# An SSM convolution in front of a gated MLP: joined products, reordered rows, a rounding moved into PSUM, and another order of the units

## The chip, the cores and the metric

The kernel runs on one core of a Trainium2 chip. TensorE (PE) multiplies matrices out of SBUF into PSUM; its weight loads are shown as an engine of their own (PEld). VectorE (DVE) and ScalarE (ACT) read and write PSUM and SBUF, GpSimd (POOL) and SyncE (SP) here mostly issue DMAs. The metric is the device time of one execution in microseconds. An execution is also profiled, and all rows below come from that one.

## The reference, cut to what matters

The input has 2048 positions and 576 channels. A first block (A) normalises each row, runs a state-space convolution along the positions and adds the result; a second block (B) is a gated MLP with a 2048x2048 mixing of the positions. Only block A is touched here.

```python
dt = exp(log_dt)[:, None];  logdA = dt * (A_re + 1j * A_im);  dB = dt * (B_re + 1j * B_im)
P  = exp(logdA[:, :, None] * arange(L))            # (576 channels, 128 states, 2048 positions)
K  = einsum("dn,dnl,dn->dl", C_re + 1j * C_im, P, dB).real
y  = irfft(rfft(pad(u)) * rfft(pad(K)))[:L] + u * Dskip     # a causal convolution per channel
...
h = layernorm(x) * (1 + ca) + sa;  x = x + ga * A(h)
h = layernorm(x) * (1 + cb) + sb;  x = x + gb * MLP(h)
```

K is a sum over 128 states of w * exp(a*l) * cos(phase*l + phi). The position l is split into a coarse and a fine part, so that K comes from products of tables. The convolution is done with a Fourier transform in stages, as matrix products.

## The kernel before, in words

The work on block A is in `ssm`, as a loop over rounds (`tick`, 0 to 39). There are 36 groups of 16 channels. In each round one group enters, and the earlier ones are each one stage further on. The units of a group g:

- `e_unit` (three groups at once, every third round): TensorE expands the logarithms of the magnitudes, a pair of products with 48 rows and 512 columns and one with 112 rows, and ScalarE takes Exp of both (lines 443 to 447) into `et`.
- `t_unit`, round g: TensorE expands the phases, counted in turns, four products of 48 rows and 256 columns into two banks of PSUM (L455). ScalarE adds a large constant, MAGIC, which rounds to whole turns (Identity, L456, into `ft`). VectorE subtracts MAGIC and the phase (L457), which leaves minus the fraction of a turn, and clears the sign into a second tile (L459).
- `s_unit`, round g+1: two Sin activations, cosine (L464) and sine (L465).
- `p_unit`, round g+2: VectorE multiplies magnitudes and phases, five instructions (L475 to L479), into `pg` and back into `et`.
- `kg_unit`, round g+3: 32 small products of 128x32 tiles into one bank (L489), copied by ScalarE with reordered columns into `kab` (L492); `d_unit` adds the skip term (L496).
- `k1_unit`, round g+4: eight products with 128x64 tiles (L506), copied by ScalarE or VectorE into `k1` (L511, L513). This is the first stage of the transform of K.

Every eight groups complete 128 channels. The input's transform runs beside it, in chunks of 512 columns. `u_unit` is one product (L548), copied by ScalarE into `ue` (L549); two DMAs of POOL's queue write `us`, the same with both halves of the partitions swapped (L551, L552). Two rounds later `z_unit` makes K's second stage (L561) and VectorE multiplies it with `ue` and with `us` (L562, L563). A round later `v_unit` transforms back with two products (L570, L571), and ScalarE's copy (L572) is stored. `y_unit` does the last stage (L615), adds x and stores.

In the first eight rounds the layer norm of block A and its first stage (`ln_pair`, L426 and L428) run in the same loop, as do the preparation of the poles and the modulation (`mod_unit`). The channel groups' pole tables (`lb`, `lc`, `la`) come by DMA from a scratch in HBM.

All these products pass through PSUM: the tiles `ps` (two, of two banks) and `pk` (four, of one bank) are handed round among the units.

What sets the order: the loop's text gives each instruction its priority, and inside the loop a scheduler puts each engine's instructions in order at build time, so they may stand otherwise than in the text. Instructions that are issued through a helper (line 145) keep the text's order; these are the parts ahead of the loop and all of the MLP behind it. Each engine then runs its list in order.

The text of a round before:

```python
go(z_unit); lag(p_unit, 2); lag(t_unit, 0); lag(s_unit, 1); go(v_unit)
lag(kg_unit, 3); go(u_unit); lag(k1_unit, 4); go(y_unit); lag(d_unit, 3)
# every third round: e_unit for three groups
```

Of the kernel before, what the change touches and what calls it, by code (L numbers as in the profile page):

```python
# [31 lines left out]
def consts():  # L32
# [64 lines left out]
    sel = np.zeros((112, 1536))  # L97
    sel[:48, :1024] = sel[64:, :1024] = half
    sel[:48, 1024:1280] = sel[64:, 1280:] = rge.reshape(48, 256)
    ones = np.zeros((128, 128))  # L100
    ones[::32] = 1.0
    f = np.float32
# [55 lines left out]
def ssm(tc, I, x1_d, consts_s, dram, mod_d, mlp):  # L158
# [5 lines left out]
    with ExitStack() as ctx:  # L164
# [22 lines left out]
        sel = tb.tile([112, 1536], BF, name="sel", bufs=1)  # L187
# [194 lines left out]
        def ln_stats(i):  # L382
            x = x4s[i]
            nm = ep.tile([128, 4], F32, name="nm")
            r = ep.tile([128, 4], F32, name="r")
            if i < 2:
                junk = ep.tile([128, 4, HC], F32, name="st1o").rearrange("p (a b) d -> p a (b d)", a=2)
                ss = ep.tile([128, 4], F32, name="ss")
# [48 lines left out]
        def e_unit(g):  # L437
            c, gi = divmod(g, 9)
            lb = lt["lb", c]
            e = et[g] = tb.tile([128, 1536], F32, name="et", bufs=5)  # L440
            pa = ps2()
            for h, (l, r) in enumerate(zip(halves(lb, gi), rows(256, 512))):
                T.matmul(pa[:, h], l, r, start=True, stop=True)
            A.activation(e[:, :1024].rearrange("p (h n) -> p h n", h=2), pa, AF.Exp)
            pb = ps1()
            T.matmul(pb, lb[:, gi], sel[:, 1024:], start=True, stop=True)
            A.activation(e[:, 1024:], pb, AF.Exp)

        def t_unit(g):
# [3 lines left out]
            for k, (n, c0) in enumerate((("lc", 768), ("la", 0))):  # L453
                for h, (l, r) in enumerate(zip(halves(lt[n, c], gi), rows(c0, 256))):
                    T.matmul(pa[:, h].rearrange("p (c k j) -> p k c j", c=8, k=2)[:, k], l, r, start=True, stop=True)  # L455
            A.activation(f, pa, AF.Identity, bias=magic)  # L456
            V.scalar_tensor_tensor(f, f, MAGIC, pa, op0=ALU.subtract, op1=ALU.subtract)  # L457
            ct = tb.tile([128, 2, 512], F32, name="ft", bufs=5)
            V.tensor_single_scalar(ct.bitcast(I32), f.bitcast(I32), 0x7FFFFFFF, op=ALU.bitwise_and)  # L459
            tt[g] = (f, ct)  # L460

        def s_unit(g):
            f, ct = tt[g]
            A.activation(ct, ct, AF.Sin, bias=halfpi, scale=-TWO_PI)  # L464
            A.activation(f, f, AF.Sin, scale=-TWO_PI)  # L465

        def p_unit(g):

            f, ct = tt[g]
            e = et.pop(g)  # L470
            p = tb.tile([128, 1536], F32, name="pg")
            pr, pi = [t[:, :1024].rearrange("p (c s j) -> p c s j", c=16, s=2) for t in (p, e)]
            gr, gi = [t[:, 1024:].rearrange("p (c a) -> p c a", c=16) for t in (p, e)]
            c3, s3 = [x.rearrange("p h (c k j) -> p k (h c) j", c=8, k=2) for x in (ct, f)]
            V.tensor_tensor(gr, gi, c3[:, 1], op=ALU.mult)  # L475
            V.tensor_tensor(pr, pi, c3[:, 0, :, None, :].to_broadcast([128, 16, 2, 32]), op=ALU.mult)
            V.tensor_tensor(gi, gi, s3[:, 1], op=ALU.mult)
            V.scalar_tensor_tensor(pi[:, :, 0], s3[:, 0], -1.0, pi[:, :, 0], op0=ALU.mult, op1=ALU.mult)
            V.tensor_tensor(pi[:, :, 1], s3[:, 0], pi[:, :, 1], op=ALU.mult)  # L479
            tt[g] = (pr, pi, gr, gi)  # L480

        def kg_unit(g):
            pr, pi, gr, gi = tt.pop(g)
            pm = ps1()
            for i in range(4):
                for x_, y_, st in ((gr, pr, True), (gi, pi, False)):
                    for j in range(4):
                        c = 4 * i + j
                        T.matmul(pm[32 * j:32 * j + 32, 64 * i:64 * i + 64], x_[:, c], y_[:, c].rearrange("p s j -> p (s j)"),  # L489
                                 start=st, stop=not st, skip_group_check=True)  # L490
            kk = kab[g] = tb.tile([128, 4, 64], F32, name="kab")
            A.activation(kk.rearrange("p i (b w) -> p i w b", w=4), pm[:, :256].rearrange("p (i w b) -> p i w b", i=4, w=4), AF.Copy)  # L492

        def d_unit(g):
            kk = kab[g]
# [34 lines left out]
        def part(n, bufs=2):  # L530
            return sb.tile([128, 512], F32, name=n, bufs=bufs)

        def by(t, c):
            return t.rearrange("p (k d) -> p k d", d=CHW[c])

# [7 lines left out]

        def u_unit(c, i):
            u1 = st.pop((c, i))
            ue = part("ue", 4)
            pm = ps1()
            T.matmul(pm, fwd, u1, start=True, stop=True)  # L548
            A.activation(ue, pm, AF.Copy)  # L549
            us = part("us", 4)  # L550
            G.dma_start(us[:64], ue[64:])  # L551
            G.dma_start(us[64:], ue[:64])  # L552
            st[c, i] = (ue, us)

        def z_unit(c, i):
            ue, us = st.pop((c, i))
            w = CHW[c]
            za, zb = part("za"), part("zb")
            pm = ps1()
            for j, k in enumerate(range(32)[kr(c, i)]):  # L560
                T.matmul(pm[:, w * j:w * j + w], cst[k // 8][:, k % 8], k1t[c][:, k, :w], start=True, stop=True)  # L561
            V.tensor_tensor(za, pm, ue, op=ALU.mult)  # L562
            V.tensor_tensor(zb, pm, us, op=ALU.mult)  # L563
            st[c, i] = (za, zb)

        def v_unit(c, i):
            za, zb = st.pop((c, i))
            v = part("ue", 4) if c == NC - 1 and i > 1 else part("v")
            pm = ps1()
            T.matmul(pm, inva, za, start=True, stop=False)  # L570
            T.matmul(pm, invb, zb, start=False, stop=True)  # L571
            A.activation(v, pm, AF.Copy)  # L572
            G.dma_start(v_d[c][:, kr(c, i)], by(v, c))

        def y_vload(c, q):
# [1 line left out]
            w = CHW[c]  # L577
            rows = v_d[c].rearrange("(b h g) k d -> b h (g k) d", b=16, h=2)[bs].rearrange("b h p d -> p h b d")
            if c == NC - 1:
                t = part("ue", 4)  # L580
                st["yv", c, q] = t[:, :4 * w], t[:, 4 * w:]
                for hh in range(2):
                    S.dma_start(by(t[:, 4 * w * hh:4 * w * hh + 4 * w], c), rows[:, hh])
                return
            if c == NC - 2 and q < 2:
                vt = [part("za"), part("zb")]
            else:
                vt = [part("u1", 5)[:, :4 * w] for _ in range(2)]
            st["yv", c, q] = vt
# [3 lines left out]
        def y_xload(c, q):  # L593
# [3 lines left out]
            elif c == NC - 1:  # L597
                xb = mlp.x1l[:, 4 * q - 4:4 * q]
            else:
                xb = by(part("us", 4) if c == NC - 2 or (c, q) == (2, 3) else part("xb"), c)  # L600
                S.dma_start(xb, I["x"][:, bs, chan(c)])
            st["y", c, q] = xb, bs

# [68 lines left out]
        for tick in range(NG + 4):  # L672
# [25 lines left out]
                    e_unit(g)  # L698
            go(y_load)
            go(u_load)  # L700
            go(z_unit)
            lag(p_unit, 2)
            lag(t_unit, 0)
            lag(s_unit, 1)
            go(v_unit)
            lag(kg_unit, 3)
            go(u_unit)
            lag(k1_unit, 4)
            go(y_unit)
            lag(d_unit, 3)  # L710
            if tick == 0:
                T = nc.tensor
            if tick % 3 == 0 and 0 < tick < NG:
                for g in range(tick, tick + 3):
                    e_unit(g)
            if tick < 5:
                next(p1, None)
                next(p1, None)
# [1449 lines left out]
```

## Time and profile before

| what | us |
|---|---|
| time, median of three runs (1782.43 to 1786.51) | 1784.2 |
| the profiled execution | 1784.31 |
| its span, first to last instruction | 1782.5 |
| TensorE busy | 1664.0 (93%) |
| VectorE busy | 1265.7 (71%) |
| ScalarE busy | 854.0 (48%) |
| POOL busy | 247.4 (14%) |
| DMA | 376.04 MB, mean 211 GB/s |

Busy shares are means over very different stages: block A with its preparation runs from 0 to about 410 us, the MLP's first phase to about 712, its second to the end. A view by windows shows each stage by itself. A row of a group gives line, engine, operation, what it writes and reads, sizes and count, then its busy time and the mean time of one in ns, and the idle time of the engine ahead of it with what ended it. A busy TensorE counts a product from start to end although products overlap, so the distance from start to start is what a product costs in a dense stream.

### The profile page before, as it was taken

The numbers are of one execution on the slowest core, as the hardware profiler recorded it, in microseconds if no ns is written. First come the engines' busy times: TensorE is split into PE (matmuls) and PEld (weight loads), VectorE is DVE, ScalarE is ACT, GpSimd is POOL, SyncE is SP. The second block draws the span as 40 slices with busy tenths as digits, with TensorE's granted clock in tenths as the row PEclk, the third lists the DMA queues.
The fourth block names the chain that finished last, engine by engine and source line by source line (L and its number), as shares of the span: only waits on it lengthen the run. The fifth ranks groups of instructions, "written<-read, shape, count | busy, mean of one in ns | idle before, by whom it ended". The sixth has DMA issues, their size and how long they took to land.

```text
span 1782.5 us, 36327 instructions
## 1 busy us (share of the span) xinstructions
PE 1664.0 (93%) x15094; PEld 1239.3 (70%) x15094; DVE 1265.7 (71%) x2331; ACT 854.0 (48%) x1130; POOL 247.4 (14%) x400
## 2 busy tenths in 40 slices
PE   4487899997899999999989999999999999999999
PEld 1243455565455545777877888888888888888887
DVE  6864999966999998788899777688344478344432
ACT  5877999854477666455434444234232223122210
POOL 4311232333122211000000000000111100111100
PEclk8586999998999999999999999999999999999999
DMA  9356645579689779777665886773766572556531
GB/s 276 117 175 202 175 124 167 167 210 301 210 251 293 243 227 268 279 250 254 234 215 163 285 301 236 268 247 121 251 222 231 196 233 99 192 195 218 192 111 40
DMA packets 183380, 376.04 MB, mean 211 GB/s; under 512 B 39360, under 2 KB 103488, under 8 KB 182448
## 3 DMA queue, kind: packets, MB, share of 16 engines
q1 hardware_dynamic: 140416, 175.05, 32.2%
q0 software_dynamic: 36896, 172.01, 28.7%
q10 hardware_dynamic: 5904, 26.67, 3.7%
q8 instruction: 118, 1.93, 0.4%
q14 instruction: 46, 0.38, 0.1%
HBM read 262.93 MB, written 101.31 MB: 204 GB/s over the span
## 4 chain that ended last, share of the span: by engine, by line
PE 57%; DVE 14%; DMA 5%; issue 3%; ACT 1%; POOL 0%; SPq 0%; ACTq 0%; DVEq 0%; POOLq 0%
PE ps L145 54%; DVE bsz L145 2%; DMA zset<-set_d 2%; DMA wsst<-in_w_spT 1%; DVE zset L145 1%; DVE gt L145 1%; DVE n L145 1%; DVE rq L145 1%; DVE wsp L145 1%; PE pk L145 1%; DVE wso L145 1%; DVE raw L145 1%; DVE nt L145 1%; DMA z_d<-z 1%; PE pk L561 1%
## 5 line engine op out<-in xcount | busy, mean ns | idle before, releaser
L145 PEld LDWEIGHTS <-zset 128*128 128x128 f16 x7182 | 701.9, 98 | 93.9 <-DVE zset L145 8.8
L145 PE MATMUL ps<-wsp,zset 128*128 128x256 f16 x6048 | 667.7, 273 | 8.4 <-DVE zset L145 6.8
L145 PE MATMUL pz<-wz,nt 128*128 128x512 f16 (+1 forms) x1120 | 222.3, 358 | 10.6 <-DVE nt L145 4.5
L145 ACT ACTIVATE z<-gt 128x1024 f16<-128x1024 f32 x56 | 59.0, 1054 | 281.7 <-DVE gt L145 281.7
L145 PEld LDWEIGHTS <-nt 128*128 128x128 f16 x1120 | 108.8, 98 | 117.9 <-DVE nt L145 5.9
L145 DVE SCALAR_TENSOR_TENSOR gt<-ps,sc,bsp 128x512 f32<-128x512 f32 x36 | 27.0, 749 | 204.8 <-PE ps L145 203.0
L1876 POOL DMA_DIRECT2D zset<-set_d x96 | 51.0, 532 | 870.5 <-PE ps L145 623.2
L145 PE MATMUL ps<-wout,z 128*128 128x288 f16 x1344 | 170.0, 286 | 0.0
L145 PEld LDWEIGHTS <-z 128*128 128x128 f16 x1344 | 131.5, 98 | 33.0
L145 PE MATMUL ps<-n2o,zset 128*128 128x256 f16 x1134 | 128.2, 273 | 0.0
L145 DVE SCALAR_TENSOR_TENSOR gt<-ps,sc,gt 128x512 f32<-128x512 f32 (+1 forms) x180 | 122.2, 696 | 7.9 <-DVE gt L145 0.5
L145 DVE TENSOR_TENSOR raw<-raw 128x512 f32<-128x512 f32 (+2 forms) x228 | 119.1, 528 | 10.6 <-DMA raw<-z_d 6.3
L145 ACT ACTIVATE zset<-raw 128x1792 f16<-128x1792 f32 x48 | 81.2, 1691 | 63.2 <-PE ps L145 39.5
L145 DVE TENSOR_TENSOR zset<-raw,zset 128x1792 f16<-128x1792 f32 x48 | 97.0, 2020 | 17.4 <-ACT zset L145 16.2
L145 DVE TENSOR_TENSOR z<-ps,z 128x512 f32<-128x512 f32 (+1 forms) x126 | 72.0, 598 | 36.8 <-ACT z L145 25.1
L145 ACT ACTIVATE wsp<-raw,sc 128x1792 f16<-128x1792 f32 x25 | 44.6, 1785 | 42.9 <-DVE raw L145 35.2
L145 ACT ACTIVATE z<-z,sc 128x1024 f32<-128x1024 f32 x21 | 24.1, 1148 | 75.6 <-DVE z L145 71.9
L457 DVE SCALAR_TENSOR_TENSOR ft<-ft,ps 128x1024 f32<-128x1024 f32 x36 | 43.7, 1214 | 22.4 <-ACT ft L456 22.4
L145 ACT ACTIVATE z<-z,nm,r 128x1152 f32<-128x1152 f32 x24 | 31.4, 1342 | 51.1 <-DVE nm L145 30.5
L145 ACT ACTIVATE z<-pz,sc 128x512 f32<-128x512 f32 (+1 forms) x96 | 51.5, 584 | 8.8 <-DMA z_d<-z 4.8
L145 PE MATMUL ps<-n2q,wf 128*128 128x512 f16 x252 | 55.7, 379 | 0.0
L506 PEld LDWEIGHTS pk<-small,kab 128*64 128x64 f32 x576 | 34.2, 145 | 28.9 <-issue 17.3
(359 smaller groups left out, 2507.6 us busy)
## 6 DMA issues: line engine op xcount, KB each, us to landing
zset<-set_d POOLq DMA_DIRECT2D x96, 896.0 KB, 4.9
raw<-z_d SPq DMA_DIRECT2D x48, 512.0 KB, 5.5
set_d<-zset ACTq DMA_DIRECT2D x24, 896.0 KB, 6.0
z_d<-z POOLq DMA_DIRECT2D x32, 576.0 KB, 9.0
zset<-wa_d POOLq DMA_DIRECT2D x18, 896.0 KB, 4.9
raw<-in_w_spT SPq DMA_DIRECT2D x25, 512.0 KB, 4.8
set_d<-zset SPq DMA_DIRECT2D x12, 896.0 KB, 5.9
u_d<-st1o POOLq DMA_DIRECT2D x16, 576.0 KB, 4.0
```

The lines of the kernel that those rows point to most:

```text
L145: return self.tc.keep_in_program_order(f(*a, **k))
L457: V.scalar_tensor_tensor(f, f, MAGIC, pa, op0=ALU.subtract, op1=ALU.subtract)
L506: T.matmul(pm[64 * ri:64 * ri + 64, 128 * i:128 * i + 128], kk[:, i], r1[ri], start=True, stop=True, skip_group_check=True)
L561: T.matmul(pm[:, w * j:w * j + w], cst[k // 8][:, k % 8], k1t[c][:, k, :w], start=True, stop=True)
L1876: self.nc.gpsimd.dma_start(o, self.set_d[f, j - 1] if j else self.wa_d[f])
```

## The change: what it does

- In `t_unit`, the first ten groups (NR = 10) do the rounding with products: a product of ones with a row that holds MAGIC puts MAGIC into PSUM, the phases are added, MAGIC is taken off by a product with minus ones, and the phases are subtracted. VectorE copies the result. The other groups keep Identity and subtraction. The table `sel` grows from 1536 to 2368 columns for it.
- Cosine and sine lie in one tile (`ft`, three buffers of twice the size in place of five).
- In `p_unit`, the two products with the fine table become one, with the magnitude broadcast. Both results lie in `pg`, which is larger.
- `ue` and `us` become halves of one tile `uu`, `za` and `zb` of `zz`, and the two products in `z_unit` become one with K's bank broadcast.
- The rows of the table `c_st` stand in another order, so that `kab` is copied without reordering columns.
- `ss` has one buffer.
- From the tenth round on the units of a round are given in another order.

```diff
-    st2 = np.stack([forward(-2 * np.pi * np.outer(b4, k + 0.25 + 32 * k2) / 2048) for k in range(32)], 1)
+    st2 = np.stack([forward(-2 * np.pi * np.outer(b, k + 0.25 + 32 * k2) / 2048) for k in range(32)], 1)
...
         def t_unit(g):
-            f = tb.tile([128, 2, 512], F32, name="ft", bufs=5)
+            cs = tb.tile([128, 2, 2, 512], F32, name="ft", bufs=3)
+            ct, f = cs[:, 0], cs[:, 1]
             pa = ps2()
...
+            def magics(c0, start):
+                for h, (l, r) in enumerate(zip(rows(c0, 128), rows(2048, 64))):
+                    T.matmul(pa[:, h].rearrange("p (c j) -> p c j", c=8), l, r[:, None, :].to_broadcast([48, 8, 64]), start=start, stop=False,
+                             skip_group_check=True)
+            if g < NR:
+                magics(2112, True)
+                phases((768, 0), False, False)
+                magics(2240, False)
+                phases((1536, 1792), False, True)
+                V.tensor_copy(f, pa)
+            else:
+                phases((768, 0), True, True)
+                A.activation(f, pa, AF.Identity, bias=magic)
+                V.scalar_tensor_tensor(f, f, MAGIC, pa, op0=ALU.subtract, op1=ALU.subtract)
...
         def p_unit(g):
-            V.tensor_tensor(gr, gi, c3[:, 1], op=ALU.mult)
-            V.tensor_tensor(pr, pi, c3[:, 0, :, None, :].to_broadcast([128, 16, 2, 32]), op=ALU.mult)
-            V.tensor_tensor(gi, gi, s3[:, 1], op=ALU.mult)
+            V.tensor_tensor(gri, e[:, None, 1024:].rearrange("p x (c a) -> p x c a", c=16).to_broadcast([128, 2, 16, 32]), cs[:, 1], op=ALU.mult)
+            V.tensor_tensor(pr, pi, c3[:, :, None, :].to_broadcast([128, 16, 2, 32]), op=ALU.mult)
...
         def kg_unit(g):
-            A.activation(kk.rearrange("p i (b w) -> p i w b", w=4), pm[:, :256].rearrange("p (i w b) -> p i w b", i=4, w=4), AF.Copy)
+            A.activation(kk, pm[:, :256].rearrange("p (i b) -> p i b", i=4), AF.Copy)
...
         def z_unit(c, i):
-            V.tensor_tensor(za, pm, ue, op=ALU.mult)
-            V.tensor_tensor(zb, pm, us, op=ALU.mult)
+            V.tensor_tensor(zz, pm[:, None, :].to_broadcast([128, 2, 512]), uu, op=ALU.mult)
...
+            if tick < 10:
...
+            else:
+                go(z_unit)
+                lag(p_unit, 2)
+                lag(t_unit, 0)
+                lag(s_unit, 1)
+                lag(kg_unit, 3)
+                lag(k1_unit, 4)
+                go(y_unit)
+                go(v_unit)
+                e_one()
+                go(u_unit)
+                lag(d_unit, 3)
+                e_one()
+                e_one()
```

Here `phases` makes the four products of L455 with the given columns, flags and signs, and `e_one` gives one of the three `e_unit`s of a third round. In the first ten rounds the order is the old one.

More of the change, by code (lines that the diff above doesn't have):

```diff
@@ L96, in consts @@
     half = np.concatenate([rgt.reshape(48, 256), rpe.reshape(48, 512), rpt.reshape(48, 256)], axis=1)
-    sel = np.zeros((112, 1536))
+    sel = np.zeros((112, 2368))
     sel[:48, :1024] = sel[64:, :1024] = half
-    sel[:48, 1024:1280] = sel[64:, 1280:] = rge.reshape(48, 256)
+    for h in range(0, 112, 64):
+        rows = slice(h, h + 48)
+        sel[rows, 1536:1792] = -half[:, 768:]
+        sel[rows, 1792:2048] = -half[:, :256]
+        sel[h, 2048:2112] = MAGIC
+        sel[rows, 2112:2240] = 1.0
+        sel[rows, 2240:] = -1.0
+    sel[:48, 1024:1280] = sel[64:, 1280:1536] = rge.reshape(48, 256)
     ones = np.zeros((128, 128))
@@ L186, in ssm @@
         tb = tabs.enter_context(tc.tile_pool(name="tb", reuse_waits="tile", bufs=2))
-        sel = tb.tile([112, 1536], BF, name="sel", bufs=1)
+        sel = tb.tile([112, 2368], BF, name="sel", bufs=1)
         dsk = tb.tile([128, 144], F32, name="dsk", bufs=1)
@@ L456, in t_unit, with phases @@
-            A.activation(f, pa, AF.Identity, bias=magic)
-            V.scalar_tensor_tensor(f, f, MAGIC, pa, op0=ALU.subtract, op1=ALU.subtract)
-            ct = tb.tile([128, 2, 512], F32, name="ft", bufs=5)
+            def phases(cols, start, stop):
+                for k, (n, c0) in enumerate(zip(("lc", "la"), cols)):
+                    for h, (l, r) in enumerate(zip(halves(lt[n, c], gi), rows(c0, 256))):
+                        T.matmul(pa[:, h].rearrange("p (c k j) -> p k c j", c=8, k=2)[:, k], l, r, start=start, stop=stop, skip_group_check=True)
@@ L531, in part, with half @@
             return sb.tile([128, 512], F32, name=n, bufs=bufs)
+        spare = []
+        def half():
+            if not spare:
+                uu = sb.tile([128, 2, 512], F32, name="uu", bufs=4)
+                spare.extend((uu[:, 1], uu[:, 0]))
+            return spare.pop()
         def by(t, c):
@@ L579, in y_vload @@
             if c == NC - 1:
-                t = part("ue", 4)
+                t = half()
                 st["yv", c, q] = t[:, :4 * w], t[:, 4 * w:]
@@ L585, in y_vload @@
             if c == NC - 2 and q < 2:
-                vt = [part("za"), part("zb")]
+                zz = sb.tile([128, 2, 512], F32, name="zz")
+                vt = [zz[:, 0], zz[:, 1]]
             else:
@@ L599, in y_xload @@
             else:
-                xb = by(part("us", 4) if c == NC - 2 or (c, q) == (2, 3) else part("xb"), c)
+                xb = by(half() if c == NC - 2 or (c, q) == (2, 3) else part("xb"), c)
                 S.dma_start(xb, I["x"][:, bs, chan(c)])
```

83 lines of the change are left out of this document (42 added, 41 removed).

## The prediction

> **What bounds the kernel now.** I read the table of time windows first, to find how much of the execution the edited code fills, then the waits of each engine inside that part, then the costs of single groups. The windows (columns: length, busy time of each engine with its instruction count, granted TensorE clock, DMA share, GB/s):
>
> ```profile
> core 0: us, PE busy (x) PEld busy (x) DVE busy (x) ACT busy (x) POOL busy (x), PEclk, DMA share, GB/s
> 0.00:54.00 54.00, 21.94 (x109) 7.93 (x110) 37.16 (x108) 32.65 (x65) 18.15 (x33) 0.83 0.83 237
> 54.00:178.00 124.00, 88.34 (x1218) 45.70 (x1218) 83.67 (x187) 94.86 (x128) 29.71 (x44) 0.66 0.55 172
> 178.00:372.00 194.00, 177.40 (x2554) 106.40 (x2552) 176.96 (x267) 180.79 (x233) 58.97 (x99) 0.97 0.58 162
> 372.00:410.00 38.00, 37.83 (x416) 24.11 (x416) 22.04 (x37) 14.15 (x22) 15.28 (x27) 1.00 0.85 221
> 410.00:712.00 302.00, 279.52 (x1571) 152.92 (x1569) 265.65 (x779) 191.54 (x284) 64.70 (x84) 0.97 0.83 256
> ```
>
> Everything edited lies in the first 410 us, the SSM. Rounds 0 to 9 of its loop are the stretch from 54 to 178, rounds 10 to 35 run from 178 to 410. From 178 to 372 three engines are busy 91 to 93% of the time, so no busy share names the bound; the waits do. First TensorE's from 178 to 372, then its longest from 54 to 178, then VectorE's longest in both stretches (columns: who waited for whom, us in total, times, longest):
>
> ```profile
> PE pk L561 <- ACT v L572: 5.8, 6, 1.5
> PE ps L443 <- ACT et L444: 2.8, 4, 0.9
> PE ps L443 <- DVE ft L457: 2.8, 2, 2.3
> PE pk L506 <- ACT ue L549: 1.8, 1, 1.8
> PE pk L561 <- ACT k L513: 0.9, 1, 0.9
> PE pk L615 <- DVE k L511: 0.9, 2, 0.4
> PE pk L561 <- DVE k L511: 0.4, 1, 0.4
> ```
>
> ```profile
> PE ps L426 <- ACT st1o L428: 18.2, 8, 5.1
> PE pk L446 <- DMA lb<-pb_d: 8.4, 1, 8.4
> PE ps L455 <- ACT st1o L428: 4.1, 2, 3.8
> ```
>
> ```profile
> DVE ft L457 <- ACT ft L456: 15.0, 4, 8.3
> DVE pg L475 <- ACT ft L464: 15.8, 6, 5.9
> ...
> DVE ft L457 <- ACT ft L456: 11.5, 6, 4.1
> ```
>
> From 178 to 372 TensorE waits 5.8+2.8+2.8+1.8+0.9+0.9+0.4 = 15.4 us in all; the other 179 us it works back to back. So **TensorE is the bound of rounds 10 to 35**, and 15.4 us is the most that faster neighbours can give back; 11.3 of it is owed to ScalarE. From 54 to 178 the picture is another: TensorE waits at least 22.3 us for ScalarE, VectorE 30.8 us for it, and ScalarE is the fullest engine (94.9 of 124). There **ScalarE bounds**, beside an 8.4 us wait for a load, with TensorE granted 0.66 of its clock. From 372 on TensorE alone bounds.
>
> **The change, part by part.** The prices (columns as on the page: busy us, mean ns of one, idle before; stretch 178 to 372 except the last two, which are of 54 to 178 and of the whole execution):
>
> ```profile
> L492 ACT ACTIVATE kab<-pk 128x256 f32<-128x256 f32 x25 | 16.2, 650 | 2.9 <-PE pk L489 2.9
> L476 DVE TENSOR_TENSOR pg<-et,ft 128x1024 f32<-128x1024 f32 x25 | 30.4, 1215 | 0.0
> L475 DVE TENSOR_TENSOR pg<-et,ft 128x512 f32<-128x512 f32 x26 | 17.8, 685 | 6.3 <-PE pk L489 4.3 <-ACT ft L464 2.0
> L477 DVE TENSOR_TENSOR et<-et,ft 128x512 f32<-128x512 f32 x25 | 17.0, 680 | 0.0
> L562 DVE TENSOR_TENSOR za<-pk,ue 128x512 f32<-128x512 f32 x24 | 16.4, 682 | 1.4 <-PE pk L561 1.0
> L563 DVE TENSOR_TENSOR zb<-pk,us 128x512 f32<-128x512 f32 x24 | 16.3, 678 | 1.0 <-DMA us<-ue 1.0
> L456 ACT ACTIVATE ft<-ps,consts_s 128x1024 f32<-128x1024 f32 x10 | 11.1, 1114 | 1.6 <-PE ps L455 1.6
> L145 ACT ACTIVATE z<-ps 128x256 f32<-128x256 f32 x42 | 13.5, 372 | 7.5 <-PE ps L145 7.5
> ```
>
> *Joined products.* Two products of 685 and 680 ns become one of 1024 columns, for which the one of 1215 ns stands: 0.15 us saved in each round. The two of z, 682 and 678, save the same: together 0.30 us of VectorE per round, 26 rounds, 7.8 us. The joined p product reads cosine and sine, so it waits for both Sin activations where the first used to wait for one; in the built order the 1024-column product that needs the cosine alone stands ahead of it in several rounds. The joined z product waits for the swapped half; a rival below.
>
> *Reordered rows.* kab is written straight instead of with a step of four: 256 columns out of PSUM straight take 372 ns (last row) against 650. That is 0.28 us of ScalarE per round, 36 rounds: about 2.2 us in the eight that fall in the early stretch, 7.2 later. Bounds: nothing, and 0.28.
>
> *First ten groups rounded in PSUM.* Ten Identity activations of 1114 ns go from ScalarE: 11.1 us. The subtraction on VectorE becomes a plain copy of the same 1024 columns out of PSUM; I count it equal. TensorE gets, for each of ten rounds, two more pairs of 512-column products and two more pairs of 256. At the low clock (first fence) and at the full one (second), the columns being start, busy, instruction:
>
> ```profile
> 42.06 0.61 PE L145 MATMUL ps<-sel,lb 48*128 48x512 bf16 x2
> 42.60 0.61 PE L145 MATMUL pk<-sel,lb 112*128 112x512 bf16 x1
> ...
> 62.80 0.40 PE L455 MATMUL ps<-sel,lc 48*128 48x256 bf16 x2
> 62.99 0.42 PE L455 MATMUL ps<-sel,la 48*128 48x256 bf16 x2
> ```
>
> ```profile
> 329.33 0.39 PE L443 MATMUL ps<-sel,lb 48*128 48x512 bf16 x2
> 329.65 0.39 PE L446 MATMUL pk<-sel,lb 112*128 112x512 bf16 x1
> ...
> 330.30 0.61 PE L446 MATMUL pk<-sel,lb 112*128 112x512 bf16 x2
> 330.74 1.06 PE L561 MATMUL pk<-k,cst 128*128 128x128 f32 x8
> ```
>
> From start to start a 512 pair takes 0.54 us at the low clock, a 256 pair 0.19: 2x0.54 + 2x0.19 = 1.5 us a round, 15 us for ten, as the upper end. At the full clock a product of 512 takes 0.22 (the two at 330.30 last 0.44), so some 0.66 a round, 7 us. With the granted 0.66 I take 10 us. What hides it: TensorE's 22 us of waits for ScalarE in this stretch, and ScalarE now has 11.1 + 2.2 = 13.3 us less to do. Ends: 13.3 us won if all of TensorE's addition falls into its waits, 10 us lost if none does and TensorE paces. TensorE's busy time would be 88.3 + 10 = 98 us, more than ScalarE's remaining 81.6: the bound passes to TensorE, so only a little is left. I take 3 us won; the 8.4 us wait for lb stays, as that load is issued behind the last row store on POOL's queue, and moves along with it.
>
> *The order from the tenth round.* A change of tile shape costs TensorE 0.10 us: 0.32 from the 48x512 pair to the 112x512 product, against 0.22 within one shape. As the units are now written, a round without e has four changes of shape in place of six (u no longer stands between kg and k1), which would save 2x0.10x26 = 5.2 us. But the scheduler gives TensorE another order than the text: it puts t into the middle of the kg products and u among the e units. Counted in the built programs, three rounds have 19 changes of shape before and 19 after, and the whole of rounds 10 to 37 has 176 before and 169 after. So **the grouping is worth 7x0.10 = 0.7 us**. The Trainium skill says, on its page "TensorEngine Tiling (Array Packing)", section Key Properties, that changing the tiling mode, as opposed to the tile, drains the engine. The 0.10 us in the rows is such a drain; by that rule and the order as written the gain would be the 5.2 us, by the built order it is the 0.7.
>
> What the neighbours give back in rounds 10 to 35: ScalarE, the engine that TensorE waits for, has 0.28 us less in each of 26 rounds, 7.2 us, and VectorE 7.8 at the same time. The two run side by side and TensorE's waits come to 15.4. I take 6.3, a bit under ScalarE's 7.2, as some waits are of one round's order and not of its load. Ends: 0 and 15.4.
>
> *Start.* sel grows from 112x1536 to 112x2368 two-byte elements, 186 KB more in SP's queue ahead of the loads that TensorE waits for; at the 237 GB/s of the first window 0.8 us lost. Nothing hides that, since TensorE waits for small and the modulation weights there. The tail from 372 to 410 is TensorE's alone and doesn't change.
>
> Sum: +0.8 - 3.0 - 6.3 - 0.7 = -9.2 us. What follows is bound by VectorE and TensorE (265.7 and 279.5 of 302 us), with DMA at 0.83; I let 1 us be lost there to loads that land no earlier. So -8.2: the profiled execution took 1784.31 us, 0.1 over the median of 1784.2, and the forecast is **1776 us**.
>
> **The rivals.** *A: TensorE paces the early rounds.* It bounds rounds 0 to 9 with the low clock, and all 10 to 15 us of its added products count. For it: the 98 us of busy time above, and a clock of 0.66. Against: 22 us of waits beside it. It decides from the point at which more than about 8 us of the added work stays outside the waits. With 12 of it exposed: 0.8 + 12 - 7 = +6, 1790 us.
>
> *B: the swap comes late.* u is now given at the end of the round, behind k1, y and v, and the joined z product needs both halves. Where slack was least before:
>
> ```profile
> 336.19 1.12 PE L548 MATMUL pk<-u,small 128*128 128x512 f32 x2
> 342.35 0.53 POOL L552 DMA_DIRECT2D us<-ue  x1
> DMA to landing us min/median/max: 2.2/4.3/8.1
> 348.38 0.68 DVE L562 TENSOR_TENSOR za<-pk,ue 128x512 f32<-128x512 f32 x1
> ```
>
> The second swap is issued at 342.9 and lands, at the median, at 347.2, 1.2 us ahead of the product. u moves later in its round by the k1 and y products that now pass it, but its activation no longer stands behind three Exp pairs, only behind one. A loss begins once the landing is over 1.2 us later; a wait of 1.5 us in the 8 rounds with e costs 12 us: about 1788 us.
>
> *C: the gains cancel.* TensorE's own 179 us is the floor, its waits only change names, and the early rounds come out even: 1784 us.
>
> *D: the clock.* In the first 178 us the granted clock is 0.66 to 0.83, later 0.97 and more. More products in the early rounds could raise it. At 0.85 instead of 0.66 TensorE's 98 us shrink to 76, ScalarE's 81.6 with the load wait of 8.4 and the rest would bound, and some 14 us rather than 3 are won there: 1765 us. The Trainium skill has a rule for this ("TensorE: Matmul & The Clock Gate", The HAM clock gate: half rate by default, full rate after a busy window of about 3.4 us); by it the early rounds should run at full rate wherever TensorE is dense, which this row of the early stretch doesn't bear out, with 0.50 granted at 11.4 of 11.9 us busy:
>
> ```profile
> 136.60:148.50 11.90, 11.37 (x138) 5.50 (x139) 5.76 (x10) 11.85 (x17) 1.51 (x2) 0.50 0.37 141
> ```
>
> **How the numbers follow.** Forecast 0.50 (its own range 1768 to 1780.5), A 0.15, B 0.10, C 0.13, D 0.12. Two executions of this kernel can't be told apart within 0.2%, 3.6 us. Faster: forecast and D, 0.62; same: C, 0.13; slower: A and B, 0.25. The range for 8 in 10 goes from D's 1765 to A's 1790, with both ends of the early rounds in it.
>
> **What would show it.** In the profile after: joined products near 1.21 us and kab near 0.37; Identity x26; TensorE's waits in rounds 10 to 35 at about 9 us instead of 15.4, with the same number of shape changes; the early stretch 3 us shorter with TensorE busier than ScalarE; the first products of mod 0.8 us later. It would be wrong if the joined z product waited for the swap, if the early stretch grew, or if kab stayed at 0.65.

## The result and the profile after

The changed kernel takes 1781.0 us (median of 20 executions, 1774.4 to 1784.5), the kernel before 1786.5 beside it (20 executions, 1782.4 to 1792.4). The ratio is 0.9967, 95% interval 0.9959 to 0.9976: 5.9 us faster, 4.3 to 7.3. The forecast was 8.2 us faster. In absolute terms 1781.0 lies half a microsecond above the forecast's own range (1768 to 1780.5) and well inside its range for 8 in 10 (1765 to 1790); the kernel before, too, took 2.3 us more here than the 1784.2 that the forecast started from.

The profiled execution of the changed kernel took 1784.37 us, nearly the longest of its 20, and the profiled one of before 1784.31. So the ends of the two traces say nothing of the gain, and stretches of them are of use only as far as they repeat. The windows after (columns as before):

```profile
0.00:54.00 54.00, 22.62 (x105) 8.31 (x106) 34.00 (x105) 28.97 (x61) 18.10 (x33) 0.84 0.90 240
54.00:178.00 124.00, 93.63 (x1318) 48.08 (x1318) 86.49 (x180) 85.27 (x122) 30.85 (x46) 0.71 0.55 166
178.00:372.00 194.00, 178.34 (x2628) 112.75 (x2629) 177.87 (x223) 175.91 (x234) 56.80 (x98) 0.98 0.59 171
372.00:410.00 38.00, 38.00 (x359) 25.29 (x356) 17.96 (x23) 11.51 (x20) 16.54 (x27) 1.00 0.91 250
```

In the early stretch ScalarE is down from 94.9 to 85.3 us, TensorE up from 88.3 to 93.6, and TensorE is the fuller one. From 178 to 372 ScalarE falls by 4.9 us while TensorE hardly moves. The waits of TensorE in that stretch, us in total, times, longest:

```profile
PE ps L450 <- ACT et L451: 5.0, 7, 0.8
PE pk L592 <- ACT k L537: 4.9, 1, 4.9
PE pk L592 <- ACT kab L516: 3.6, 4, 0.9
PE pk L580 <- ACT kab L516: 1.1, 1, 1.1
PE pk L530 <- DVE kab L520: 0.2, 1, 0.2
```

That is 14.8 us, against 15.4 before; 4.9 of it is one single wait, at the first product of z. The largest wait of before, for v's copy, is gone, and others stand in its place. The single instructions came out as priced (groups of the stretch 178 to 372, the copy of 54 to 178):

```profile
L501 DVE TENSOR_TENSOR pg<-et,ft 128x1024 f32<-128x1024 f32 x26 | 31.7, 1218 | 3.5 <-ACT ft L489 3.5
L593 DVE TENSOR_TENSOR zz<-pk,uu 128x1024 f32<-128x1024 f32 x25 | 30.5, 1218 | 2.2 <-PE pk L592 2.2
L516 ACT ACTIVATE kab<-pk 128x256 f32<-128x256 f32 x26 | 9.9, 382 | 1.4 <-PE pk L513 1.4
L479 DVE COPY ft<-ps 128x1024 f32<-128x1024 f32 x10 | 12.2, 1217 | 13.2 <-PE ps L467 13.2
```

A joined product takes 1.22 us (forecast 1.21), kab 0.38 (0.37). The work that was to go, went; what it is worth is another matter.

### The profile page after: what moved, and what is told of

It is laid out like the page before. It is cut to its first block, busy times and chain, and to the rows that moved or that the text cites. A ratio compares the mean times of both kernels' runs of the same rounds, so it can differ in the third digit from the quotient of the medians.

```text
span 1782.6 us, 36406 instructions
## 1 busy us (share of the span) xinstructions
PE 1669.4 (94%) x15174; PEld 1247.6 (70%) x15174; DVE 1259.5 (71%) x2259; ACT 832.1 (47%) x1118; POOL 244.5 (14%) x400
## 4 chain that ended last, share of the span: by engine, by line
PE 65%; DVE 14%; DMA 7%; ACT 5%; issue 5%; POOL 2%; SPq 1%; ACTq 0%; DVEq 0%; POOLq 0%
PE ps L152 53%; PE pz L152 2%; DVE zset L152 2%; PE pk L513 2%; DVE bsz L152 2%; PE pk L530 2%; DMA wsst<-in_w_spT 1%; PE pk L592 1%; DVE gt L152 1%; DMA ln_x<-in_x 1%; DMA zset<-set_d 1%; PE pk L600 1%; DVE wsp L152 1%; DVE n L152 1%; DVE rq L152 1%
## 5 line engine op out<-in xcount | busy, mean ns | idle before, releaser
L152 ACT ACTIVATE z<-pz,sc 128x512 f32<-128x512 f32 (+1 forms) x96 | 51.7, 581 | 13.1 <-PE pz L152 7.1
L501 DVE TENSOR_TENSOR pg<-et,ft 128x1024 f32<-128x1024 f32 x36 | 43.8, 1217 | 12.8 <-ACT ft L489 12.7
L152 DVE BATCH_NORM_STATS2 bsz<-z 128x6 f32<-128x384 f32 x96 | 48.4, 546 | 6.2 <-ACT z L152 5.8
```

Source lines behind the costliest of these rows:

```text
L152: return self.tc.keep_in_program_order(f(*a, **k))
L501: V.tensor_tensor(pr, pi, c3[:, :, None, :].to_broadcast([128, 16, 2, 32]), op=ALU.mult)
```

## The experiments

Every ratio is against the kernel before, run on the same chip beside it. The intervals are about ±0.0012 (±2 us) each, so a difference of two ratios is known to some 3 us; where one question was asked in several settings, the mean is better. Four kernels (no rounding the second time, the large sel, the later load with the old order, rounding alone) ran on another chip than the other eight, so a difference across the two chips also assumes that an edit is worth the same on both.

**The order undone.** The changed kernel with the old order of units in all rounds.

```diff
-            if tick < 10:
+            if True:
```

> The changed kernel with the old order of units in all rounds. Theory (the order is worth little: 7 changes of tile shape at 0.10 us): within 2 us of the changed kernel, ratio to before 0.996 to 0.998, K's last k1 product no more than 2 us later than in the changed kernel. Rival (the order carries the gain, whatever the number of shape changes, by taking the waits out of TensorE's queue): 4 us or more slower than the changed kernel, ratio 0.999 to 1.001.

1786.2 us, ratio 0.9996 (0.9985 to 1.0006). Without the new order nothing of the gain is left. The forecast's largest term, 6.3 us of relief by ScalarE and VectorE, should have remained here.

**The order alone.** The kernel before, with only the units from the tenth round on in the new order.

```diff
             else:
...
+                lag(kg_unit, 3)
+                lag(k1_unit, 4)
+                go(y_unit)
+                go(v_unit)
+                e_one()
+                go(u_unit)
```

> The kernel before with nothing changed but the order of the units from the tenth round on: four product pairs, the step of four in kab and the 1536-column sel stay as they were. Theory 1 (the order carries the gain by itself): it gives what separates the kernel after from the one with the old order, about 5 us, and pays nothing at the start: 1781 to 1782, ratio 0.997. Theory 2 (the order only pays because the joined products and the straight kab made room on VectorE and ScalarE): no gain without them, 1786 to 1787, ratio 0.9995 to 1.0005.

1783.4 us, 0.9982 (0.9968 to 0.9996). The order gains without the joined products and the short kab, so its gain doesn't hang on the room that they make.

**Joined products and kab alone.** The old order everywhere, no rounding in PSUM, the small sel.

```diff
-        NR = 10
+        NR = 0
...
-            if tick < 10:
+            if True:
```

> Only the joined products and the straight kab: the old order of units everywhere, no group rounded in PSUM, sel with its 1536 columns. Theory of the forecast (ScalarE and VectorE relieve TensorE from the tenth round): 6 us or more faster than before, 1780, ratio 0.9965, since the price of the larger sel is not paid either. Rival (TensorE's waits only change their owner, as in the old-order run, and the early rounds gain some 4 us from the shorter kab and products while the start keeps its cost): 1783 to 1786, ratio 0.998 to 1.0. On the start: if the larger sel is what delays it, the first product of sel comes at 42 as in the kernel before; if it is something else, at 45.

1785.95 us, 0.9993 (0.9977 to 1.0008): the rival holds. The two parts that take the most instructions' time away are worth nothing that can be told from zero. (The joined tiles ft, pg, uu and zz and the single buffer of ss come with them and were not priced apart.) Its first product of sel comes at 43.5, so small sel goes with an early start.

The traces show why, since these rounds repeat almost exactly. Rows of TensorE (start, busy, instruction, idle before and releaser) in the kernel after, then with the order alone, over one cycle of three rounds (the first product of z of a round, the 129th in all, to that of three rounds later):

```profile
306.46 1.16 PE L592 MATMUL pk<-k,cst 128*128 128x128 f32 x8
314.44 1.16 PE L592 MATMUL pk<-k,cst 128*128 128x128 f32 x8 [0.90 <-ACT kab L516]
321.14 1.05 PE L592 MATMUL pk<-k,cst 128*128 128x128 f32 x8
329.23 0.39 PE L450 MATMUL ps<-sel,lb 48*128 48x512 bf16 x2 [0.71 <-ACT et L451]
329.72 1.16 PE L592 MATMUL pk<-k,cst 128*128 128x128 f32 x8
```

```profile
309.85 1.16 PE L561 MATMUL pk<-k,cst 128*128 128x128 f32 x8
318.09 1.16 PE L561 MATMUL pk<-k,cst 128*128 128x128 f32 x8 [1.16 <-ACT kab L492]
324.78 1.05 PE L561 MATMUL pk<-k,cst 128*128 128x128 f32 x8
332.88 0.39 PE L443 MATMUL ps<-sel,lb 48*128 48x512 bf16 x2 [0.71 <-ACT et L444]
333.37 1.16 PE L561 MATMUL pk<-k,cst 128*128 128x128 f32 x8
```

The rounds last 7.98, 6.70 and 8.58 us with the joined products and the short kab, and 8.24, 6.69 and 8.59 without. The 0.27 us that each kab became shorter appears in one round of three, as 0.26 less of one wait; in the other two kab was never waited for. In the cycles before and behind this one (from the 105th and from the 153rd product of z) it isn't waited for at all, and they last 23.07 and 24.05 us in both kernels. The wait of 0.71 is the same to 0.01 us: TensorE waits there until the Exp of an earlier pair (L451, L444) has read the banks that the next pair writes, and this doesn't shrink when ScalarE has less to do elsewhere.

The same stretch, from the first product of z to the 257th of 320, in four kernels. After, then old order, then order alone (its first row is cut off at 190 us by the view), then the kernel before once more:

```profile
184.07 2.07 PE L592 MATMUL pk<-k,cst 128*128 128x128 f32 x8 [4.86 <-ACT k L537]
405.12 1.90 PE L152 MATMUL pk<-k,cst 128*128 128x64 f32 x16
```

```profile
186.80 2.07 PE L592 MATMUL pk<-k,cst 128*128 128x128 f32 x8 [0.33 <-ACT k L537]
409.29 1.97 PE L152 MATMUL pk<-k,cst 128*128 128x64 f32 x16
```

```profile
188.69 1.65 PE L561 MATMUL pk<-k,cst 128*128 128x128 f32 x6 [0.75 <-ACT k L513]
409.12 1.89 PE L145 MATMUL pk<-k,cst 128*128 128x64 f32 x16
```

```profile
180.48 2.07 PE L561 MATMUL pk<-k,cst 128*128 128x128 f32 x8 [0.92 <-ACT k L513]
403.06 1.97 PE L145 MATMUL pk<-k,cst 128*128 128x64 f32 x16
```

The lengths are 221.0 and 220.4 us with the new order (after, order alone), 222.5 and 222.6 with the old one. All 12 executions traced with one of these two orders fall the same way: six with the old order 222.0 to 224.0, mean 222.9; six with the new one 219.9 to 221.0, mean 220.4. The order gives 2.5 us here. Joining the products and straightening kab gives 0.0 under the new order (220.4 against a mean of 220.4 for the five executions that have them) and 0.6 under the old (222.6 against 223.2).

This stretch begins with 3 to 6 us at half clock, which differ from trace to trace. From the 25th product of z to the 257th TensorE does the same number of products of every unit in all twelve, and eleven are at full clock throughout (the first profile of before, which the table leaves out, is granted 0.50 once more, from 315.2 to 318.6):

| kernel | 25th to 257th product of z (us) | TensorE's gaps in it (us) |
|---|---|---|
| old order, not joined (before once more, rounding alone) | 200.5, 201.1 | 10.1, 10.3 |
| old order, joined products and kab (three kernels) | 201.3 to 201.8 | 10.3 to 10.6 |
| new order, not joined (the order alone) | 198.9 | 10.0 |
| new order, joined products and kab (five kernels) | 197.88 to 197.91 | 9.0 to 9.1 |

So here joining and kab take 1.0 us off under the new order, which is four waits shortened by about 0.26, and nothing under the old. The new order takes off 3.7 us with them and 1.9 without. Of the 3.7, about 1.4 are waits, and 4 changes of tile shape fewer (152 in place of 156) make 0.4; the rest, near 2 us, is time in which TensorE is busy in both, and what it is stays open.

**TensorE held to the order of the text.** From the tenth round TensorE's instructions are pinned in the order in which the units are given.

```diff
+            if tick == 10:
+                T = mlp.tied.tensor
```

> The changed kernel with TensorE's instructions kept in the text's order from the tenth round on, so that the grouping really takes place: 156 changes of tile shape where the changed kernel has 169 and the kernel before 176. Theory (shape changes cost 0.10 us each): 1.3 us won by them, and possibly more lost where a product now waits in the queue ahead of ready ones; total within 4 us of the changed kernel. Rival (grouping is the large part that the scheduler undid): 4 us or more faster than the changed kernel.

1780.8 us, 0.9967 (0.9955 to 0.9979), the same as the kernel after, with 156 changes of shape from round 10 to 37 in place of 169. A further 13 changes less, 1.3 us at 0.10 each, bring nothing: between the kg products of groups 10 and 35 TensorE now waits 13.1 us (sum of the gaps in the trace) in place of 9.9. From the 25th to the 257th product of z its trace takes 201.2 us, as long as with the old order, though the time is that of the kernel after; where it makes this up isn't settled.

**Only u moved.** The new order, but v left at its old place behind s.

```diff
                 lag(s_unit, 1)
+                go(v_unit)
                 lag(kg_unit, 3)
                 lag(k1_unit, 4)
                 go(y_unit)
-                go(v_unit)
                 e_one()
```

> The kernel after, but from the tenth round on v stays at its old place behind s, and only u is moved behind y (so kg, k1 and y still stand together, and the e units stand as in the old order, at the end). Theory 1 (what counts is that u no longer stands between kg and k1): as the kernel after, 1780 to 1782, ratio 0.997. Theory 2 (what counts is that v, e and u are spread between products that ScalarE must evict, so that no three Exp pairs stand in a row): as the kernel with the old order, 1786, ratio 0.9995 to 1.0005. In between, the gain is shared.

1782.1 us, 0.9974 (0.9959 to 0.9988). That can't be told from the kernel after, and lies below the old order (0.9996), though the two intervals touch. (Unlike what is expected above, one e unit still stands ahead of u here; only v differs from the kernel after.) In its trace the stretch from the first to the 257th product of z is 222.4 us, as long as with the old order, but the granted clock is 0.50 once more in it, from 307.8 to 311.2. From the 25th product on it is 199.3 us. Such a step of half clock is what the first profile of before has there and its second hasn't, 202.1 against 200.5; less these 1.6 us this kernel would be at an estimated 197.6, as with the new order. So the place of u, with one e unit ahead of it, seems to be what counts, and v's place to add little; one trace doesn't prove it.

**No rounding in PSUM**, with the small sel; run twice, once more in the second time for its start.

```diff
-        NR = 10
+        NR = 0
```

> The changed kernel with Identity and subtraction in all groups, and sel at its old 1536 columns. Theory (the rounding in PSUM pays 3 us in the early rounds and costs 3.7 us at the start by the bigger table): same time as the changed kernel within 1.5 us; the first product with sel back at about 42 us instead of 45.8. Rival 1 (the rounding carries the gain): 3 us or more slower than the changed kernel. Rival 2 (it only costs, as TensorE paces the early rounds): 3 us or more faster.

> The kernel after without rounding and with the small sel once more, as the partner of the run with the large sel. Its first execution had its first product of sel at 45.3, though the load is the old size. Theory 1 (size decides): 42 to 43.5 this time, the first look was chance. Theory 2 (something else that the kernels of the new order have in common): 45 again. Time 1781 to 1783.5 by both.

1782.1 us, 0.9977 (0.9964 to 0.9989), and 1780.3, 0.9968 (0.9957 to 0.9978). So rounding, as the change loads it, is worth about 1 us, within the error of zero.

**No rounding, but the large sel loaded.**

> The kernel after without rounding in PSUM in any round, but with the large sel of 2368 columns loaded at the head all the same: what is left is the price of the 186 KB by themselves. Theory 1 (the size of the load is what delays the start, and the delay reaches the end): first product of sel at 45.5 to 46, and slower than the same kernel with the small sel (1782.1) by 2 to 5 us: 1784 to 1787. Theory 2 (the start scatters from one execution to the next, and 186 KB cost the 0.8 us of the forecast): within 1.5 us of the same kernel with the small sel.

1782.5 us, 0.9974 (0.9962 to 0.9985): against the mean of the two runs with the small sel (0.9972) the 186 KB cost 0.3 us of time, as theory 2 has it. But its start is late: first product of sel at 45.9.

**The columns for rounding loaded later**, by an issue of their own behind dsk.

```diff
-        S.dma_start(sel, I["c_sel"])
+        S.dma_start(sel[:, :1536], I["c_sel"][:, :1536])
...
+        S.dma_start(sel[:, 1536:], I["c_sel"][:, 1536:])
```

> The changed kernel, but the new columns of sel are loaded by a transfer of their own behind the layer norm's loads on SP's queue. Theory (the bigger table delays the loads behind it): the first product with small back near 23.4 us instead of 25.0, the first with sel near 42 instead of 45.8, and the total 2 to 4 us less than the changed kernel, ratio 0.994 to 0.996. Rival (the start's delay has another cause, such as the one buffer for ss or chance in the transfers): the first product with sel stays at 45 us or later and the total stays.

1774.9 us, 0.9933 (0.9921 to 0.9945): 12 us under the kernel before and 6 under the one after. It beats both, and by more than the 2 to 4 us expected. The first product of sel in the kernel after, in this one, and in the first run without rounding:

```profile
45.77 0.61 PE L152 MATMUL ps<-sel,lb 48*128 48x512 bf16 x2
```

```profile
43.01 0.61 PE L152 MATMUL ps<-sel,lb 48*128 48x512 bf16 x2
```

```profile
45.27 0.61 PE L152 MATMUL ps<-sel,lb 48*128 48x512 bf16 x2
```

Over all traces: with 2368 columns in one load this product starts at 45.6 to 46.0 (five executions), with 1536 in the first load at 42.1 to 43.5 (eight), and once, in the last row, at 45.3. In the six late starts VectorE waits 1.9 to 3.1 us for a table of the poles whose load is queued on SP behind sel, in the eight early ones 0.5 at most. The row of after:

```profile
DVE t_q L152 <- DMA t_n_B_im<-in_A_B_im: 3.1, 1, 3.1
```

**The later load with the old order.** The same edit and the old order in all rounds.

> The kernel after with the columns for rounding loaded by a later issue of their own, and the old order of units in all rounds. If the parts add up: the old order costs 5.5 us and the later load wins 6, so 1780 to 1781, ratio 0.9965. If the later load only pays with the new order (a delay at the start is caught up elsewhere under the old one): 1784 to 1786.

1779.9 us, 0.9961 (0.9949 to 0.9973). The parts add up: the order is worth 5.0 us here, and the later load 6.3.

**Rounding alone**, with the later load; four product pairs, kab with its step, the old order.

```diff
-            A.activation(kk, pm[:, :256].rearrange("p (i b) -> p i b", i=4), AF.Copy)
+            A.activation(kk.rearrange("p i (b w) -> p i w b", w=4), pm[:, :256].rearrange("p (i w b) -> p i w b", i=4, w=4), AF.Copy)
```

> Rounding of the first ten groups in PSUM alone, with its columns loaded by the later issue: four product pairs instead of the joined products, kab with its step of four, the old order of units. Theory of the forecast (ScalarE bounds the early rounds, 11.1 us of Identity activations leave it, TensorE takes on 10 us of products, most of which falls into its waits): 3 us faster than before, 1782 to 1784, ratio 0.998. Rival A (TensorE paces the early rounds): 1788 and more. If rounding is what pays most when its load is out of the way: 1779 to 1781, ratio 0.9965, and the joined products and kab add nothing beside it.

1782.0 us, 0.9964 (0.9952 to 0.9977): rounding by itself, its load out of the way, gains 6.4 us, which by its ratio is the last of the cases expected. Its early stretch, and TensorE's longest waits in it:

```profile
54.00:178.00 124.00, 94.18 (x1311) 48.48 (x1311) 88.27 (x193) 87.85 (x123) 30.75 (x46) 0.74 0.59 179
```

```profile
PE ps L433 <- ACT st1o L435: 12.7, 8, 4.3
PE ps L450 <- DVE et L504: 4.9, 1, 4.9
PE ps L433 <- DVE ft L479: 3.1, 2, 1.7
```

The wait for the row copies (st1o) is down from 18.2 to 12.7 us and of the phases' 4.1 for them 0.3 is left; 3.1 for the new copy and 4.9 for a product come in. In the kernel before once more these two waits are 18.3 and 1.5, so the fall of the first is clear of chance and most of that of the second is not. The wait of 8.4 us for lb is 0.7 here, but 7.6 in the kernel after and 6.9 in both others with the later load. TensorE's busy time grows by 5.8 us while it also does 93 instructions more in the same 124 us.

**The kernel before once more.**

> The kernel before once more, unchanged. If the profiled start is reproducible, the first product of sel comes at 42.0 to 42.5 and the last st1o copy at 153.5 to 154.5, and the ratio is 1.000 within 0.1%. If the start differs from one execution to the next by 1 us and more, the shift of 3.7 us seen in one execution of the kernel after is partly chance.

1787.9 us, 1.0008 (0.9994 to 1.0022). But its profiled execution reaches the kg products of group 10 at 191.8, 4.9 us earlier than the first profile of the same program. The two agree to 0.4 us up to 110 us. Three windows of the first profile, then of this one:

```profile
110.00:115.00 5.00, 3.96 (x66) 2.09 (x57) 1.08 (x3) 3.36 (x6) 1.31 (x2) 1.00 0.99 338
115.00:120.00 5.00, 1.66 (x13) 0.63 (x16) 5.00 (x17) 2.20 (x3) 0.76 (x1) 0.72 0.80 240
120.00:125.00 5.00, 5.00 (x29) 1.74 (x22) 5.00 (x14) 1.42 (x4) 0.00 (x0) 0.50 0.32 120
```

```profile
110.00:115.00 5.00, 4.45 (x59) 2.61 (x56) 2.10 (x8) 3.04 (x5) 1.31 (x2) 0.75 1.01 363
115.00:120.00 5.00, 3.73 (x39) 1.71 (x37) 5.00 (x16) 2.55 (x4) 0.76 (x1) 0.91 0.86 276
120.00:125.00 5.00, 4.57 (x97) 2.68 (x98) 5.00 (x13) 4.96 (x7) 0.52 (x1) 1.00 0.09 35
```

In one execution TensorE is granted 0.50 from 120 to 125 and issues 29 products, in the other 1.00 and 97. The clock falls in both, only at other times: the next stretch at half is from 117.2 to 127.5 us in the first, from 112.5 to 115.9 in the second. In the same few microseconds ScalarE waits for a store of the row copies, 4.3 us in the first and 3.0 in the second. Which of the two made the difference isn't settled. So in the early rounds a difference of 5 us between two single traces proves nothing, and what the parts are worth there is taken from the medians.

**The sum of the parts**, each the mean over the settings in which it was taken, at 1786.5 us:

| part | settings (us) | mean |
|---|---|---|
| order from the tenth round | -5.2, -5.0, -3.7, -3.2 | -4.3 |
| joined products and kab | -1.3, -0.5, -1.7 | -1.2 |
| rounding, its columns loaded later | -6.4, -5.7, -7.1 | -6.4 |
| these columns at the head instead | +6.1, +6.3 | +6.2 |
| sum | | -5.7 |
| measured | | -5.9 |

The order was taken with rounding, with rounding and the later load, without rounding, and alone; joined products and kab alone, beside rounding, and beside the order; rounding alone, beside the joined products, and beside these and the order. Such differences, added up along a chain of kernels from before to after, give the measured gain whatever they are, so the sum is no test. That a part comes out much alike in several settings is one.

## Why the prediction was nearly right, and by the wrong terms

**The sum** was -8.2, measured -5.9. The four terms that make up its -9.2 were off by 3 to 5 us each, in both directions, and cancelled; that the sum came near is luck.

**Relief in rounds 10 to 35: -6.3 forecast, -1.2 measured at most.** This is the step that failed. "TensorE waits 15.4 us, 11.3 of it for ScalarE, and ScalarE gets 7.2 us less to do" took a sum of waits as if it were a backlog. The bounds named were 0 and 15.4, and a value near ScalarE's saving was taken "as some waits are of one round's order and not of its load". Nearly all of them are: they stand at fixed places of a three-round cycle. Of the instructions that became shorter only kab stands in front of one, four times in the stretch, which is the 1.0 us found there under the new order. After the change TensorE waits 14.8 us where the forecast wanted about 9. Without the single 4.9 it would be 9.9, but that isn't the relief that was meant: over the same products the table above has 10.1 to 10.3 us of gaps with nothing joined and 10.3 to 10.6 with everything joined under the old order, 10.0 with the order alone, and 9.0 only where both stand together. Rival C said just this (its waits only change names) and was right for these rounds.

**Order: -0.7 forecast, -4.3 measured** (the intervals allow 2.7 to 5.9). The price of 0.10 us for a change of shape holds. With the old order and all else as after, the round that is without e runs like this:

```profile
315.26 1.16 PE L592 MATMUL pk<-k,cst 128*128 128x128 f32 x8 [0.38 <-ACT v L602]
322.06 1.16 PE L592 MATMUL pk<-k,cst 128*128 128x128 f32 x8
```

It takes 6.80 us with four changes of shape, against 6.70 with three in the new order (314.44 to 321.14 above). The Trainium skill's rule ("TensorEngine Tiling (Array Packing)", Key Properties: a change of tiling mode drains TensorE) agrees with that 0.10. So the counted 7 changes are 0.7 us, as forecast. What was missed is that moving units also moves who waits for whom: by the distances of z's products in the two traces, the three rounds from the 105th product on went from 24.0 us, 1.4 of it gaps, to 23.1 with 0.8, and the three from the 153rd on from 25.9, again with 1.4, to 24.0 with none; the cycle shown above is 0.1 longer than with the old order. From the 25th to the 257th product, at full clock, the traces place 3.7 us (1.9 without the joined products), of which the waits are 1.4; that is all of the 4.3 within its error. What the order does beside shortening waits and saving changes of shape, the runs don't tell.

**Early rounds: -3.0 forecast, kab's 2.2 us there included.** Rounding is worth 6.4 with its load out of the way. In that run TensorE's busy time in the early stretch grew by 5.8 us where 10 was forecast, at a granted clock of 0.74 in place of 0.66, while its wait for the row copies fell by 5.5. Rival A, that TensorE paces these rounds at 1790 us, is excluded by the run with rounding alone (at most 0.9977 of before, 1782.4). Rival D saw that the granted clock rises, 0.66 to 0.71 after and 0.74 with rounding alone; but one run without rounding had 0.72 and the kernel before, once more, 0.69, so how much of the 6.4 is the clock stays open. For the early stretch the forecast was of the right sign and half the size.

**Start: +0.8 forecast, +2.9 at the first product of sel, and +6.2 in the time.** "186 KB at 237 GB/s" counted the bytes alone. TensorE's wait for small did grow by these 0.8 us, from 9.3 to 10.1; but what lies behind sel on SP's queue (small, and the seven pole tables) comes late one by one, and TensorE and VectorE wait for one after another: for the modulation weights 6.0 us in place of 4.6, for the pole table 3.1. Why the time loses 6 us where the start loses 3, and loses nothing measurable when the same load is made without rounding, isn't settled. The run with the small sel that started late once shows that its size isn't the only thing that decides.

**Rival B, the late swap**, did not happen: no wait for uu's swapped half stands among TensorE's, and zz waits 2.2 us in all, for TensorE.

**Later phases.** The 1 us allowed for them can't be seen: from the MLP's first half-precision product to the 701st, about 450 to 603 us, the profiled execution of after takes 152.7 us and the first profile of before 149.1, but the other twelve traces lie anywhere from 148.1 to 151.7.

## What to carry to other kernels

A sum of short waits in a periodic schedule is no stock that a faster neighbour gives back: take one period, look which instruction stands in front of each wait, and count a saving only where the shortened instruction is that one. A constant needed only later doesn't belong into the load that the first instructions stand behind; here an issue of its own was worth as much as the whole change. And where one execution's trace can be 5 us off another's, single parts are priced by undoing them in more than one setting.

## What the runs showed that was not expected

Two executions of one program differ by 5 us in the early rounds, though they agree to 0.4 us up to 110. In the record of the granted clock of all 14 traces every change falls on a grid of 3.41 us, and the place of this grid against the start of the program differs from trace to trace, by 1.3 us between these two. So the same work meets a change of clock at another point each time. The Trainium skill ("TensorE: Matmul & The Clock Gate", in the part on the HAM clock gate) says that the activity window is free-running, so that what a kernel meets depends on its phase; these traces agree with that. Its rule of full rate after a busy window does not fit the first of the two: from 120.6 to 124.0 lies one whole step of the grid inside the window in which TensorE is busy for 5.00 of 5.00 us, and 0.50 is granted until 127.5.

Behind the early rounds the opposite holds: with the clock at 0.97 to 1.00 a cycle of three rounds repeats from kernel to kernel to 0.01 us, and the stretch from the 25th to the 257th product of z to 0.03 in five kernels, so there a single trace can price a change of 0.1 us, as long as its clock has no further step.
